# Block-sparse attention and an MLP mixer on one core: zero products in TensorE's gaps up to the first MLP, all transposes on TensorE, block sums by halving, and a new order of all steps

## The chip, the core and the metric

The kernel runs on one core of a Trainium2 chip. A core has five engines that run side by side, each through its own list of instructions in a fixed order: TensorE (PE in the profile; PEld is its weight load), VectorE (DVE), ScalarE (ACT), GpSimd (POOL) and SyncE (SP), which here only issues DMAs. TensorE's clock has two levels, 1.2 and 2.4 GHz; the column "PEclk" is the share of the higher one that was granted. The metric is the device time of one execution in microseconds.

## The reference

Inputs are q, k and v of 4 batches, 8 heads, 768 positions and 64 elements, and four weight matrices. For every head, positions are cut into 12 blocks of 64. A query row attends to its own block and to the three blocks whose mean key has the largest product with the query, as far as they are not in the future.

```python
k_rep = k.reshape(B, H, n_blocks, block, D).mean(axis=3)
gate_scores = np.einsum('bhsd,bhnd->bhsn', q, k_rep)
gate_scores = np.where(causal, gate_scores, -1000000000.0)
top_idx = np.argsort(gate_scores, axis=-1)[..., -top_k:]
...
scores = scale * np.matmul(q, k.transpose(0, 1, 3, 2))
mask = mask & (pos[:, None] >= pos[None, :])
scores = np.where(mask, scores, -1000000000.0)
...
...
xt = x.transpose(0, 2, 1)                      # x: (batch, 768, 512)
h = np.maximum(xt @ w_tok1, 0.0) @ w_tok2      # 768 -> 256 -> 768
u = x + h.transpose(0, 2, 1)
h2 = np.maximum(u @ w_ch1, 0.0) @ w_ch2        # 512 -> 1536 -> 512
return u + h2
```

## The kernel before

The work goes in 16 pairs of heads, four pairs a batch. `pair(p)` records all steps of one pair, `mlp(b)` those of the last two matrix products of a batch, and `block_sums(b, pr)` sums keys over blocks for the four pairs of a batch at once. Nothing runs at that point: each step is an `Op` with a cost on each engine that may do it, the buffers it reads and writes, and a priority `pr`. `Plan.run` then simulates the engines with these costs and lists the steps in the order of their planned starts; that list is what each engine gets, in that order. Priorities come from a pair's due time `T(p)` (7.0 us a pair in the first batch, 13.5 behind) less an offset for each kind of step.

A pair goes as follows. q, k and v are loaded (`q32`, `k32`, `v32`, three buffers each) on SP's queue; in the first batch k, and in all batches q, in pieces of four and two row groups for each head. q is transposed on TensorE in fp32 (line 390, recorded at 479), copied out of PSUM to `QT`, and cast to fp16 by GpSimd into `QA` (line 266 is the helper that writes all such copies). In an early pair (`p < FIRST`, the first four) k goes through TensorE in fp32 too, VectorE reduces the transposed k over each block (line 449) to `ks2`, and the gate is five fp32 products (493). In the other twelve pairs GpSimd casts k to fp16 (463), a DMA transposes it into `KA` (465), VectorE copies one half and the block indicator to their places (468, 470), and the gate uses `block_sums`: one load of the batch's k, four strided reductions on VectorE (398), and a split of the sums and of q into three bf16 parts (`R`, lines 504 and 506), with 15 products (513).

The gate's scores get a bias (518 or 496), the third largest is found (523), and the comparison gives the bias `bn`, which TensorE transposes (537) into extra rows of `QA`; with the indicator in `KA` they make a score of an unselected block very negative. Then for each of the two heads: scores in three groups (559), an exponential on ScalarE (566), a triangular mask on GpSimd (574), the product with V and a column of ones (583), reciprocal and division (586, 590). The two token products follow (601, 615), `u` is their sum with x (618), and u is transposed, by TensorE (631) in the first batch and the last pair and by DMA (622) in the other eleven. `mlp(b)` multiplies u's transpose by `wc1` (651) in 96 products of 384 columns, takes the positive part, and multiplies by `wc2` (669) in 72 products of 512 columns; VectorE adds u (672) and SP stores.

Four PSUM banks, the ring `Rr` (pm in the trace), serve all products but the scores (sc). GpSimd's queue also issues the loads of the weights, from 6 us of the planned time on.

## Time and profile before

| | us |
|---|---|
| median of 3 runs | 313.56 (313.03 to 314.58) |
| profiled execution | 313.72 |
| its span, first to last instruction | 312.0 |
| TensorE busy | 263.2 |
| VectorE busy | 184.1 |
| ScalarE busy | 156.3 |
| GpSimd busy | 108.9 |

TensorE's records overlap: a product's record goes from its start to its modelled end, so a share near 100% says that the engine never ran out of products and not that it worked at its peak. What a product costs in a row of products is the distance of starts. The view of stretches gives busy time of every engine with the number of instructions; the chain of waits gives, piece by piece, what the end hung on; the timeline gives runs of like instructions, and in brackets the idle time before them and what ended it.

### The profile page before, as it was taken

What the parts mean: (1) busy time and instruction counts of PE and PEld (TensorE: products, weight loads), DVE (VectorE), ACT (ScalarE), POOL (GpSimd) and SP (SyncE); (2) the same over time, 40 slices, a digit from 0 to 9 for tenths busy, and PEclk for the clock granted to TensorE, in tenths of its full rate; (3) what the DMA queues carried; (4) which work ended last, traced back from release to release, by engine and by line L of the source; (5) the groups of instructions that cost most, each with busy time, mean ns of one, the idle gap of its engine ahead of it and who ended that gap; (6) DMA issues with size and microseconds to landing.
All of it is one profiled execution on the core that took longest, in us unless ns stands there. A gap on an engine that the chain in (4) does not pass through costs nothing.

```text
span 312.0 us, 6419 instructions
## 1 busy us (share of the span) xinstructions
PE 263.2 (84%) x2437; PEld 175.7 (56%) x2437; DVE 184.1 (59%) x540; ACT 156.3 (50%) x249; POOL 108.9 (35%) x180
## 2 busy tenths in 40 slices
PE   1668987944999887897697999997799999979994
PEld 1537665724575654555554666665575666645551
DVE  6244657497656699788899254579972653320202
ACT  2163756430584548172384537743766477344240
POOL 4325345291174717356442133343652131100000
PEclk9999979685899999999598999999999999999999
DMA  6899999649929999999998152344113121010102
GB/s 121 189 189 189 196 241 216 135 76 156 212 58 186 229 226 202 205 231 227 172 159 175 25 152 56 40 73 106 43 21 56 39 60 28 36 67 0 69 34 101
DMA packets 102071, 38.98 MB, mean 125 GB/s; under 512 B 95012, under 2 KB 98680, under 8 KB 101752
## 3 DMA queue, kind: packets, MB, share of 16 engines
q1 hardware_dynamic: 97840, 34.42, 52.1%
q0 software_dynamic: 3744, 3.93, 8.6%
q8 instruction: 19, 0.31, 0.4%
q10 hardware_dynamic: 456, 0.22, 0.3%
q14 instruction: 12, 0.10, 0.1%
HBM read 31.68 MB, written 6.29 MB: 122 GB/s over the span
## 4 chain that ended last, share of the span: by engine, by line
PE 59%; DVE 29%; ACT 4%; issue 3%; DMA 3%; POOL 1%; SPq 0%; DVEq 0%; ACTq 0%
PE pm L651 13%; PE pm L669 12%; PE sc L559 10%; DVE ksn L398 7%; PE pm L583 4%; PE pm L601 4%; PE sc L669 3%; DVE R L504 3%; PE pm L615 3%; DVE m L523 2%; PE pm L390 2%; PE sc L651 2%; PE pm L493 2%; DVE x L590 2%; ACT E L566 2%
## 5 line engine op out<-in xcount | busy, mean ns | idle before, releaser
L566 ACT ACTIVATE E<-sc 128x1024 f16<-128x1024 f32 (+1 forms) x96 | 84.3, 919 | 31.0 <-PE sc L559 29.7
L574 POOL TENSOR_SCALAR_AFFINE_SELECT E<-E 128x256 f16<-128x256 f16 x96 | 42.5, 446 | 124.4 <-ACT E L566 124.0
L651 PE MATMUL pm<-uT,wc 128*128 128x384 f16 x344 | 66.0, 330 | 3.5 <-DVE u L618 1.1
L669 PE MATMUL pm<-wc,h 128*128 128x512 f16 x240 | 60.9, 379 | 0.8 <-DVE x L590 0.8
L559 PE MATMUL sc<-QA,KA 76*128 76x512 f16 (+7 forms) x256 | 54.3, 335 | 6.2 <-DVE QA L266 4.2
L651 PEld LDWEIGHTS <-wc 128*128 128x128 f16 x384 | 36.3, 99 | 27.9 <-issue 6.3
L658 ACT ACTIVATE h<-pm 128x384 f16<-128x384 f32 x68 | 33.4, 494 | 24.3 <-PE pm L651 24.1
L266 POOL CAST QA<-QT 64x768 f16<-64x768 f32 x32 | 33.3, 1040 | 20.2 <-ACT QT L264 10.3
L559 PEld LDWEIGHTS <-KA 76*128 76x128 f16 (+1 forms) x256 | 25.7, 105 | 25.6 <-issue 8.2
L669 PEld LDWEIGHTS <-h 128*128 128x128 f16 x288 | 26.5, 98 | 24.1 <-issue 1.2
L583 PE MATMUL pm<-VA,E 128*128 128x65 f16 x672 | 29.5, 199 | 5.4 <-POOL E L574 5.2
L583 PEld LDWEIGHTS <-E 128*128 128x128 f16 x672 | 27.5, 102 | 10.8 <-POOL E L574 6.4
L672 DVE TENSOR_TENSOR os<-u,pm 128x512 f32<-128x512 f16 x20 | 13.6, 682 | 17.1 <-PE pm L669 17.1
L618 DVE TENSOR_TENSOR u<-x,pm 128x512 f16<-128x512 f16 (+1 forms) x30 | 15.3, 547 | 12.2 <-PE pm L615 12.1
L398 DVE TENSOR_REDUCE ksn<-kb 96x16 f32<-96x1024 f32 x12 | 22.4, 1893 | 0.0
L264 ACT COPY QA<-pm 12x640 f16<-12x640 f16 x18 | 12.3, 683 | 18.7 <-PE pm L537 16.8
L390 PE MATMUL pm<-id,q 128*128 128x128 f32 x96 | 16.9, 300 | 4.5 <-DMA q<-in_q_dram 3.6
L586 DVE RECIPROCAL rc<-pm 128x6 f32<-128x6 f32 x32 | 6.1, 190 | 24.2 <-PE pm L583 22.6
L605 ACT ACTIVATE h<-pm 128x256 f16<-128x256 f32 x14 | 5.4, 384 | 28.9 <-PE pm L601 28.9
L264 ACT COPY QT<-pm 128x512 f32<-128x512 f32 (+1 forms) x28 | 13.2, 495 | 12.8 <-PE pm L390 11.1
L440 POOL CAST VA<-v 128x768 f16<-128x768 f32 x16 | 14.6, 912 | 13.2 <-DMA v<-in_v_dram 7.5
L601 PE MATMUL pm<-x,w 128*128 128x128 f16 x192 | 15.1, 235 | 4.8 <-DVE x L590 4.8
(70 smaller groups left out, 318.3 us busy)
## 6 DMA issues: line engine op xcount, KB each, us to landing
v<-in_v_dram SPq DMA_DIRECT2D x16, 384.0 KB, 4.0
out_dram<-os SPq DMA_DIRECT2D x24, 256.0 KB, 2.0
k<-in_k_dram SPq DMA_DIRECT2D x24, 192.0 KB, 4.1
kb<-in_k_dram SPq DMA_DIRECT2D x3, 1536.0 KB, 9.1
q<-in_q_dram SPq DMA_DIRECT2D x32, 128.0 KB, 4.7
wc<-in_moe_w_ch_dram POOLq DMA_DIRECT2D x8, 384.0 KB, 6.3
q<-in_q_dram SPq DMA_DIRECT2D x32, 64.0 KB, 3.0
k<-in_k_dram SPq DMA_DIRECT2D x8, 128.0 KB, 3.2
```

Source lines behind the costliest of these rows:

```text
L264: e.copy(out=out, in_=in_)
L266: e.tensor_copy(out=out, in_=in_)
L390: nc.tensor.transpose(out=t[:, 128 * i:128 * i + 128], in_=src.t[:, j0 + i].rearrange("p x d -> p (x d)"), identity=i32)
L398: P.op(dve(1024), lambda i=i: nc.vector.tensor_reduce(out=ksn.t[:, 0, 16 * i:16 * i + 16], in_=kb.t.rearrange("r (t d) -> r d t", d=64)[:, ...
L559: nc.tensor.matmul(out=s.t[:, at:at + 128 * m], lhsT=KA.t[0:K, x, 128 * kk:128 * kk + 128], rhs=QA.t[0:K, x, 128 * q0:128 * (q0 + m)], sta ...
L566: nc.scalar.activation(out=E.t[:, 1024 * g_:1024 * g_ + WIDTH[g_]], in_=s.t[:, 0:WIDTH[g_]], func=AF.Exp, scale=scale)
L574: nc.gpsimd.affine_select(out=o, in_=o, pattern=[[0, 2], [1, 128]], compare_op=ALU.is_ge, fill=0.0, base=0, channel_multiplier=-1)
L583: nc.tensor.matmul(out=t[:, jq, :], lhsT=E.t[:, cc:cc + 128], rhs=VA.t[:, x, kk, :], start=(kk == 0), stop=(kk == jq))
L601: nc.tensor.matmul(out=m1.t[:, 128 * t:128 * t + 128], lhsT=w1[:, j, 128 * t:128 * t + 128], rhs=xp.t[:, j, :], start=(j == 0), stop=(j == ...
L651: nc.tensor.matmul(out=m.t[:, 0:HS], lhsT=wc1[:, c, 128 * f:128 * f + 128], rhs=uT.t[:, c, HS * i:HS * i + HS], start=(c == 0), stop=(c == ...
L658: nc.scalar.activation(out=h2.t[:, f, :], in_=m.t[:, 0:HS], func=AF.Relu)
L669: nc.tensor.matmul(out=m.t, lhsT=h2.t[:, f, 128 * jj:128 * jj + 128], rhs=wc2[:, f, :], start=(f == 0), stop=(f == NFC - 1))
```

## The change

- **Order.** The table `L` replaces the offsets of all priorities, the due times go from 7.0 and 13.5 to 6.85 and 13.33, and the planner's costs change: a factor of 1.05 on three engines, 1.15 on DMA, eight DMA lanes, other costs for single steps.
- **Zero products.** `fill` looks at each planned gap of TensorE before the first MLP product, and puts products of a zero tile with itself there (line 730), into columns of a PSUM bank that nothing reads. There are 107, 47 of them ahead of all else.
- **Early pairs.** The first eight pairs are early instead of four; `block_sums` runs for two batches instead of three.
- **Transposes.** In late pairs k is cast as before, but transposed by TensorE in fp16 (477) and copied from PSUM into both halves of `KA`. u is always transposed by TensorE (650). No DMA transposes are left. `QA` and `KA` are laid out anew, with the extra rows behind the 64 elements for both heads.
- **Loads.** k, q and v come in whole heads (445, 450). The first pair's q is issued on ScalarE's queue. The weights' loads (379) depend on the first pair's `QT`; `wc1` comes in four loads of 128 rows, all of which the first MLP product needs.
- **Block sums.** The sum over a block's 64 rows is made by halving: six adds of 2,048 down to 64 elements (414). The planner may give those of 512 and more to GpSimd.
- **Constants.** The indicator is built on GpSimd and copied by VectorE instead of loaded.

```diff
-    FIRST = PPB
+    FIRST = EARLYP                                   # 8
...
-    EARLY, PACE = 7.0, 13.5
+EARLY, PACE = 6.85, 13.33
...
-        for i in range(4):
-            P.op(dve(1024), lambda i=i: nc.vector.tensor_reduce(
-                out=ksn.t[:, 0, 16 * i:16 * i + 16],
-                in_=kb.t.rearrange("r (t d) -> r d t", d=64)[:, 16 * i:16 * i + 16, :], axis=AX.X, op=ALU.add),
-                rd=[(kb, 0)], wr=[(ksn, i)], pr=pr - 6)
+        n = 2048
+        while n >= 64:
+            c = {"DVE": (n * 1.1 + 75, n * 1.1 + 160)}
+            if n >= 512:
+                c["POOL"] = (n * 1.6 + 75, n * 1.6 + 160)
+            P.op(c, lambda e, n=n: ENG[e].tensor_tensor(out=kb.t[:, 0:n] if n > 64 else ksn.t[:, 0, :], in0=kb.t[:, 0:n], in1=kb.t[:, n:2 * n], op=ALU.add),
+                 rd=[(kb, 0)], wr=[(kb, 0)] if n > 64 else [(ksn, 0)], pr=pr - L["ks"])
+            n //= 2
...
+        for t, src, e, lead in ((k32, ks_, "SP", "kd"), (q32, qs, "ACT" if p == 0 else "SP", "qd")):
+            for x in range(2):
+                P.op({e: (500.0, 1600.0, 768 * 17.6 / 16)}, lambda x=x, t=t, src=src, e=e: ENG[e].dma_start(
+                    out=t.t[:, :, x, :], in_=src[x].rearrange("(j p) d -> p j d", p=128)), wr=[(t, x)], pr=t0 - L[lead] - (99.0 if p == 0 else 0.0))
...
-            P.op({"SP": (700.0, 2200.0, 1500.0)}, lambda: nc.sync.dma_start_transpose(
-                out=KA.t[:, 1, :].rearrange("c (j p) -> c j p", p=128), in_=k16.t.rearrange("p j c -> p (j c)")),
...
+            def ktr(t=t):
+                for j in range(NJ):
+                    nc.tensor.transpose(out=t.t.bitcast(F16)[:, 128 * j:128 * j + 128], in_=k16.t[:, j, :], identity=id16)
+            P.op(pe(*[128] * NJ), ktr, rd=[(k16, 0)], wr=[(t, 0)], pr=t0 - L["kt"])
+            for x in range(2):
+                def kev(e, t=t, x=x):
+                    copy(ENG[e], KA.t[0:64, x, :], t.t.bitcast(F16)[64 * x:64 * x + 64, 0:S])
...
+        if p == 0:
+            weights((QT, 0))
...
-        if p not in UPE:
-            P.op({"SP": (700.0, 2200.0, 1500.0)}, lambda: nc.sync.dma_start_transpose(
...
-    order = P.run(on_slot_end)
+    def fill(o, a, b):
+        if any(x.cls for x in o.bufs):
+            mlp_on.append(1)
+        n = int((b - a) / (54.0 if a > 7000.0 else 104.0) - 1.0)
+        i = min(range(len(pm)), key=lambda i: Rr.avail[i])
+        if mlp_on or n < 2 or Rr.avail[i] > a:
+            return None
+        junk = pm[i][:, 392:512]
...
+                nc.tensor.matmul(out=junk, lhsT=zero, rhs=zero[:, 0:120], start=True, stop=True)
...
+    order = P.run(on_slot_end, fill)
```

TensorE at the start, before; `id_119` is the fp32 identity, `pm` a PSUM bank, the digits after k and q number the buffer, so that k_0 and q_0 belong to the first pair:

```order
L390 MATMUL pm_115<-id_119,k_0_66 128x128 x4
L390 MATMUL pm_116<-id_119,k_0_66 128x128 x2
L390 MATMUL pm_117<-id_119,q_0_63 128x128 x4
L390 MATMUL pm_118<-id_119,q_0_63 128x128 x2
L493 MATMUL pm_115<-ks_0_147,QT_84 128x24 x5
L390 MATMUL pm_116<-id_119,k_1_67 128x128 x4
L390 MATMUL pm_117<-id_119,k_1_67 128x128 x2
L537 LDWEIGHTS bn_153
L537 MATMUL pm_118<-id_120,bn_153 128x128
```

The same engine and place after, with `id_120` the fp32 identity, between the 47 zero products that stand first and the first pair's bias transposes; further zero products stand at the marks:

```order
L730 MATMUL pm_115<-zero 128x120
L399 MATMUL pm_115<-id_120,k_0_66 128x128 x3
L399 MATMUL pm_116<-id_120,k_0_66 128x128 x3
...
L399 MATMUL pm_117<-id_120,q_0_63 128x128 x3
L399 MATMUL pm_118<-id_120,q_0_63 128x128 x3
...
L506 MATMUL pm_115<-ks_0_133,QT_84 128x24 x5
L399 MATMUL pm_117<-id_120,k_1_67 128x128 x3
L399 MATMUL pm_118<-id_120,k_1_67 128x128 x3
...
L399 MATMUL pm_116<-id_120,q_1_64 128x128 x3
L506 MATMUL pm_118<-ks_1_134,QT_85 128x24 x5
L562 MATMUL pm_115<-id_121,bn_135 64x128
```

The second pair's q transposes and its gate have moved ahead of the first pair's bias transposes; before, only its k transposes stood there, and its q behind the first scores.

VectorE where the first block sums stand, before; `ksn` holds the sums of the batch's k in `kb`, `R` the bf16 split of q, `x` the attention's result:

```order
L504 TENSOR_TENSOR R_0_86<-QT_84 128x640
L586 RECIPROCAL rc_170<-pm_117 128x6
L590 TENSOR_TENSOR x_94<-pm_117,rc_170 128x6x64
L506 TENSOR_TENSOR R_0_88<-R_0_86 128x640
L398 TENSOR_REDUCE ksn_160<-kb_74 96x16 x4
L468 COPY KA_79<-KA_79 64x768
L402 COPY ksn_160<-ksn_160 96x64
L470 COPY KA_79<-ind 12x768
L586 RECIPROCAL rc_171<-pm_115 128x6
```

VectorE where its first block sums stand after:

```order
L614 TENSOR_TENSOR x_94<-pm_117,rc_169 128x6x64
L414 TENSOR_TENSOR kb_74<-kb_74 96x1024
L642 TENSOR_TENSOR u_100<-x_94,pm_117 128x384
L642 TENSOR_TENSOR u_100<-x_94,pm_115 128x384
L688 TENSOR_TENSOR os_108<-u_99,pm_116 128x512
L414 TENSOR_TENSOR kb_74<-kb_74 96x256
L288 COPY uT_102<-pm_117 128x384
L414 TENSOR_TENSOR kb_74<-kb_74 96x128
L288 COPY KA_80<-pm_118 64x768
L414 TENSOR_TENSOR ksn_158<-kb_74 96x64
L417 COPY ksn_158<-ksn_158 96x64
```

And GpSimd ahead of and between them, where its two steps of the same sum went:

```order
L598 AFFINE_SELECT E_91<-E_91 128x2x128 x2
L414 TENSOR_TENSOR kb_74<-kb_74 96x2048
L471 CAST k_0_72<-k_2_68 128x768
L451 CAST VA_82<-v_1_70 128x12x64
L414 TENSOR_TENSOR kb_74<-kb_74 96x512
L598 AFFINE_SELECT E_92<-E_92 128x2x128 x3
```

Four reductions in one piece on VectorE, in the second batch, became two adds on GpSimd and four short ones on VectorE with other steps between them, in the third batch; two casts and three masks stand behind the first add on GpSimd.

## Rows read from the trace of the kernel before

**Rows 1.** The page's first part: busy time, share of the span, instructions.
```profile
PE 263.2 (84%) x2437; PEld 175.7 (56%) x2437; DVE 184.1 (59%) x540; ACT 156.3 (50%) x249; POOL 108.9 (35%) x180
```

**Rows 2.** Stretches: length, busy us (instructions) of each engine, granted clock, DMA share, GB/s.
```profile
0.00:33.00 33.00, 20.22 (x118) 15.26 (x119) 14.19 (x57) 12.05 (x17) 12.62 (x30) 1.00 0.94 169
33.00:79.60 46.60, 33.04 (x367) 26.54 (x365) 33.23 (x96) 21.84 (x34) 21.38 (x35) 0.76 0.93 173
79.60:142.00 62.40, 56.92 (x564) 36.96 (x563) 47.30 (x131) 36.47 (x58) 30.60 (x44) 0.99 0.93 194
142.00:169.00 27.00, 19.78 (x199) 13.78 (x197) 23.94 (x69) 14.70 (x26) 12.09 (x17) 0.87 0.95 181
169.00:272.00 103.00, 99.07 (x994) 64.80 (x995) 59.12 (x181) 59.18 (x90) 32.17 (x56) 0.98 0.27 60
272.00:312.00 40.00, 34.17 (x202) 18.35 (x200) 6.37 (x11) 12.10 (x26) 0.00 (x0) 1.00 0.14 53
```

**Rows 3.** Chain of waits: start, length in us, TensorE's pieces of one line.
```profile
39.02 1.12 PE pm L493 x10
86.19 0.87 PE sc L559 x6
87.06 0.67 PE pm L583 x21
87.73 0.65 PE pm L651 x4
89.30 0.66 PE pm L390 x6
92.57 0.67 PE pm L601 x12
95.69 1.94 PE pm L669 x9
```

**Rows 4.** TensorE's timeline at the start: start, length, what [idle before, what ended it].
```profile
5.25 1.51 PE L390 MATMUL pm<-id,k 128*128 128x128 f32 x6 [5.25 <-DMA k<-in_k_dram]
10.38 1.51 PE L390 MATMUL pm<-id,q 128*128 128x128 f32 x6 [3.62 <-DMA q<-in_q_dram]
18.86 1.46 PE L559 MATMUL sc<-QA,KA 128*128 128x512 f16 x4 [1.53 <-DVE QA L266]
```

**Rows 5.** TensorE's timeline: token products of pairs 1, 2, 4, 8, 9, 16; first MLP product.
```profile
33.04 0.84 PE L601 MATMUL pm<-x,w 128*128 128x128 f16 x12
42.81 1.07 PE L601 MATMUL pm<-x,w 128*128 128x128 f16 x12 [0.24 <-DVE x L590]
74.14 1.44 PE L601 MATMUL pm<-x,w 128*128 128x128 f16 x12 [0.81 <-DVE x L590]
79.59 1.49 PE L651 MATMUL pm<-uT,wc 128*128 128x384 f16 x4
142.25 0.83 PE L601 MATMUL pm<-x,w 128*128 128x128 f16 x12
169.14 1.13 PE L601 MATMUL pm<-x,w 128*128 128x128 f16 x12 [2.13 <-DVE x L590]
272.02 0.83 PE L601 MATMUL pm<-x,w 128*128 128x128 f16 x12
```

**Rows 6.** Timelines of VectorE and TensorE at the first block sums.
```profile
65.27 7.21 DVE L398 TENSOR_REDUCE ksn<-kb 96x16 f32<-96x1024 f32 x4
72.90 0.42 PE L403 MATMUL pm<-id,ksn 96*128 96x96 f32 x1 [3.75 <-DVE ksn L402]
```

**Rows 7.** Groups of instructions: out<-in xcount | busy us, mean ns | idle before, releaser.
```profile
L566 ACT ACTIVATE E<-sc 128x1024 f16<-128x1024 f32 (+1 forms) x96 | 84.3, 919 | 31.0 <-PE sc L559 29.7
L398 DVE TENSOR_REDUCE ksn<-kb 96x16 f32<-96x1024 f32 x12 | 22.4, 1893 | 0.0
L504 DVE TENSOR_TENSOR R<-QT 128x640 f32<-128x640 f32 x12 | 13.3, 1106 | 2.0 <-ACT QT L264 1.9
```

**Rows 8.** GpSimd's timeline: two casts of q alone, and two beside R's subtraction.
```profile
38.22 1.70 POOL L266 CAST QA<-QT 64x768 f16<-64x768 f32 x2 [0.58 <-ACT QT L264]
63.13 2.91 POOL L266 CAST QA<-QT 64x768 f16<-64x768 f32 x2 [0.34 <-ACT QT L264]
```

More of the change, by code (lines that the diff above doesn't have):

```diff
@@ L71 @@
     AHEAD = 3000.0
+    LANES = 8
+    SLOW = {"PE": 1.0, "ACT": 1.05, "DVE": 1.05, "POOL": 1.05, "SP": 1.0}
+    DMA = 1.15
     def __init__(self):
@@ L115, in start @@
             t = max(free[e], o.not_before)
+            if e in ("SP", "ACT") and len(o.cost[e]) > 2:
+                t = max(t, lanes[0])
             for d in o.deps:
@@ L145, in run @@
                         t = max(t, dma_free - self.AHEAD)
-                        if any(x[1:] < (o.pr, o.n) and x[0] <= t for x in loads):
+                        if o.pr > -50.0 and any(x[1:] < (o.pr, o.n) and x[0] <= t for x in loads):
                             continue
@@ L163, in run @@
             occ, lat = o.cost[e][:2]
+            occ, lat = occ * self.SLOW[e], lat + occ * (self.SLOW[e] - 1.0)
             o.eng, o.start = e, t
+            if e == "PE" and fill:
+                f = fill(o, free[e], t)
+                if f:
+                    f.n, f.eng, f.start, f.end = -1, e, free[e], t
+                    fillers.append(f)
             free[e] = t + occ
@@ L168, in run @@
                 begin = max(dma_free, t + occ)
-                dma_free = begin + o.cost[e][2]
+                dma_free = begin + o.cost[e][2] * self.DMA
                 o.end = dma_free + lat
+                if e != "POOL":
+                    lanes.pop(0)
+                    lanes.append(o.end)
             for b in o.bufs:
@@ L309 @@
+    zero = sb([128, 128], F16, "zero")
     id32 = sb([128, 128], FP, "id32")
     id16 = sb([128, 128], F16, "id16")
+    ind = sb([NB, S], F16, "ind")
+    warm = sb([128, 1], FP, "warm")
+    cst = sb(list(both.shape), FP, "cst")
+    cstc = nc.inline_tensor(both, name="cstc").ap()
+    gbias, own = cst[:, 0], cst[:, 1]
+    nc.vector.memset(zero, 0.0)
     nc.gpsimd.memset(id32, 0.0)
     nc.gpsimd.affine_select(out=id32, in_=id32, pattern=[[-1, 128]], compare_op=ALU.not_equal, fill=1.0, base=0, channel_multiplier=1)
[L314 to L317 removed]
@@ L354, with weight @@
     W = {}
-    def weight(name, dst, src, cost, pr):
+    HC = DC // 2
+    def weight(name, dst, src, n, each, pr, after):
         b = Buf(None)
         W[name] = (b, 0)
-        P.op(cost, lambda: nc.gpsimd.dma_start(out=dst, in_=src), wr=[(b, 0)], pr=pr, not_before=6000.0)
-    weight("w1", w1, moe_w_tok1.rearrange("(j p) t -> p j t", p=128), swdge(768, 60), 13.0)
-    weight("w2", w2, moe_w_tok2.rearrange("(g p) s -> p g s", p=128), swdge(256, 135), 14.0)
-    HC = DC // 2
-    for i in range(2):
-        for c in range(0, NCC, 2):
-            weight(("wc1", i, c), wc1[:, c:c + 2, HC * i:HC * i + HC],
-                   moe_w_ch1[128 * c:128 * c + 256, HC * i:HC * i + HC].rearrange("(g p) f -> p g f", p=128),
-                   swdge(256, 135), 18.0 + i)
@@ L369, with weights @@
-    for f in range(0, NFC, 3):
-        weight(("wc2", f), wc2[:, f:f + 3, :], moe_w_ch2[128 * f:128 * f + 384, :].rearrange("(g p) c -> p g c", p=128),
-               swdge(384, 98), 25.0 + f / 3)
-    EARLY, PACE = 7.0, 13.5
+        P.op({"POOL": (800.0, 2200.0, n * each / 16.0)}, lambda: nc.gpsimd.dma_start(out=dst, in_=src), rd=[after], wr=[(b, 0)], pr=pr)
+    def weights(after):
+        weight("w1", w1, moe_w_tok1.rearrange("(j p) t -> p j t", p=128), 768, 60, L["w1"], after)
+        weight("w2", w2, moe_w_tok2.rearrange("(g p) s -> p g s", p=128), 256, 135, L["w2"], after)
+        for c in range(NCC):
+            weight(("wc1", c), wc1[:, c, :], moe_w_ch1[128 * c:128 * c + 128, :], 128, 247, L["wc1"] + c, after)
+        for f in range(0, NFC, 3):
+            weight(("wc2", f), wc2[:, f:f + 3, :], moe_w_ch2[128 * f:128 * f + 384, :].rearrange("(g p) c -> p g c", p=128),
+                   384, 98, L["wc2"] + f / 3, after)
@@ L697, in on_slot_end, with zeros @@
             P.quota["mlp"] = 7
-    order = P.run(on_slot_end)
+    mlp_on = []
+    def fill(o, a, b):
[6 more added lines that the diff above has]
+        junk = pm[i][:, 392:512]
+        f = Op()
+        f.cost, f.pr, f.deps = {"PE": (b - a, b - a)}, 0.0, ()
+        def zeros(n=n):
+            for _ in range(n):
+                nc.tensor.matmul(out=junk, lhsT=zero, rhs=zero[:, 0:120], start=True, stop=True)
+        f.fn = zeros
+        return f
+    order = P.run(on_slot_end, fill)
     PLAN.append(P)
```

272 lines of the change are left out of this document (130 added, 142 removed).

## The prediction

> **What bounds the kernel now.** I read the busy shares first, then the stretches, then the chain of waits, then TensorE's and VectorE's timelines. TensorE is busy 84% of the span [rows 1], so the question is what it loses. I price its work at the full clock from runs of back-to-back products in the chain [rows 3]: an MLP product of the first kind 0.65/4 = 0.1625 us, of the second 1.94/9 = 0.216, a head's scores 0.87 x 2,688/2,048 columns = 1.14 (the six products of the row have 2,048 of the head's 2,688), a head's attention-times-V 0.67, a 128-column fp16 product 0.67/12 = 0.056, an fp32 transpose 0.66/6 = 0.11, an fp32 gate 1.12 a pair, and a bf16 gate 0.48 (15 products at 0.67/21). By the program's counts: 384 x 0.1625 + 288 x 0.216 + 32 x 1.14 + 32 x 0.67 + 384 token products, 80 bias and 30 u transposes at 0.056 + 120 x 0.11 + 4 x 1.12 + 12 x 0.48 = 234 us of work in 312 us. So 78 us are lost, and counting the work up to the starts in [rows 5] says where:
> - up to the first MLP product at 79.6: 33.2 of work, 46.4 lost;
> - 79.6 to 142.25: 54.8 of work, 7.9 lost;
> - 142.25 to 169.14: 16.1 of work, 10.8 lost, with VectorE busy 23.9 of 27 [rows 2];
> - 169.14 to 272.02: 96.2 of work, 6.7 lost;
> - to the end: 33.5 of work, 6.5 lost (the last sums, the last store and a gap before the last MLP).
>
> The early loss has three causes. The first scores start at 18.86 because k's transposes run at 5.25 and q's only at 10.38, when q has landed [rows 4]. TensorE is at its lower level: the clock column reads 1.00 up to 33 us, yet six fp32 transposes take 1.51 there against 0.66 later [rows 3, 4], so I go by durations; from 33 to 79.6 the grant is 0.76 [rows 2]. And VectorE sums blocks for 7.2 us from 65.27, for which TensorE waits 3.75 and the pair's token product comes at 74.14 [rows 5, 6].
>
> **TensorE's work after the change.** 24 more fp32 transposes of k cost 2.6, 48 fp16 ones 2.7, 66 more of u 3.7; four gates go from 0.48 to 1.12, 2.6. That makes 245.3. The 107 zero products are 6.0 at the full level, all ahead of the first MLP product. In the new order 49.9 of the total 251.3 stand before that product (five pairs instead of four, and the zeros) and 201.4 behind it. Before, 200.6 stood behind it. So TensorE's work from there on is the same to 1 us, and the time is that product's start plus 201.4 plus what is still lost.
>
> **The start of the first MLP.** q of the first pair is issued on ScalarE's queue beside k on SP's, and the first weight load waits for the first pair. q's transposes move from 10.38 to somewhere between 5.25 + 1.51 and there. But in the new order both transposes and the gate of the second pair stand before the first pair's bias transposes, so TensorE waits for that pair's loads and ScalarE's copies. I take 17.5 for the first scores, between 15.2 (all of the 3.6 us wait for q saved) and 18.9 (nothing). The 47 zeros ahead of the first transposes cost 47 x 0.056 = 2.6 at the full level and 2.3 times that, 6.0, at the lower; starting near 1 us they end at 7 at worst, 1.8 after k was ready, but q and not k ends that wait, so I count 0.
>
> From scores to the first token product it took 14.2 us at the lower level; the one pair that ran at the full level went from 33.04 to 42.81, 9.8 us [rows 5]. I take 9.8: 27.3. Then four pairs. A pair asks TensorE for 6.9 us there (27.4 of work between the first and fifth token products of the new order, zeros included) and ScalarE for 84.3/16 = 5.3 in exponentials alone [rows 7], with copies on top, so 6.9 is a floor; the observed 9.8 is the ceiling. VectorE's block sums are gone here, so I take 8.6, a little nearer to the ceiling, because engines in fixed order wait for each other: 34.4. With a token product and three score products behind it (0.9) the first MLP product starts at 62.6 (55.6 by the floor, 67.4 by the ceiling), 17.0 earlier than before.
>
> **What is still lost behind it.** Block sums cost VectorE 4 x 1.893 = 7.6 us a batch, three times [rows 7]. Now two batches need them, by halving. VectorE's price for a two-input fp32 step is 1,106/640 = 1.73 ns an element [rows 7]; 1,024, 256, 128 and 64 elements cost about 2.6 us, and 512 more (0.9) in one batch. Step 2,048 goes to GpSimd, which has no such row. Its casts of 768 elements, two in 1.70, give 1.1 ns and 2.2 us; VectorE's rate gives 3.5; with the slowing seen when R is subtracted beside two casts, 2.91 against 1.70 [rows 8], 6.1. I take 3.5, the price of the same operation. Masks, casts and hence attention-times-V queue behind it on GpSimd; MLP products that stand between on TensorE cover the 3.5, and without them it is 3.5 a batch, twice.
>
> The Trainium skill's page "GPSIMD Engine Reference" (section "3.1 Elementwise — side-by-side cycle accounting") gives 4,497 ns for a two-input fp32 add of 2,048 elements and keeps such adds on VectorE. That price would add 1.0 us a batch to GpSimd, and 2.0 to the sum if no cover held. No run here shows it yet.
>
> For late pairs, VectorE loses two copies into KA and the R subtractions (1.1 us for the first of two [rows 7]) in the four pairs that are now early; the transposes by DMA go, and their copies out of PSUM (two of 768 for k, two of 384 for u) fall on VectorE and ScalarE, which have room behind 169 (59 of 103 us each [rows 2]) but not before. I keep 4 of the 7.9, 4 of the 10.8 (the batch whose block sums and R steps filled VectorE, with its clock dips) and 2.5 of the 6.7: 10.5, bounds 5 and the old 25.4. The end, 6.5, is unchanged (5.5 to 7).
>
> **Sum.** 62.6 + 201.4 + 10.5 + 6.5 = 281.0 span. The profiled execution took 313.72 for a span of 312.0, 1.7 around it, so 282.7; the median of 313.56 is 0.2 lower, which I leave. A measurement of this kernel tells about 0.5% from no change.
>
> **Rivals.**
> 1. The order holds at its floor: pairs at 6.9 and 5 us lost behind: 55.6 + 201.4 + 5 + 5.5 + 1.7 = 269.2. For it: the clock should be up from the start and the block sums are gone. Against: no interval before came near 6.9. Chance 0.17.
> 2. Losses behind the first MLP stay, since the new PSUM copies take the place of the block sums and GpSimd's adds hold masks: 62.6 + 201.4 + 25.4 + 6.5 + 1.7 = 297.6. For it: VectorE is 76% busy from 79.6 to 142. Chance 0.15.
> 3. The zeros don't do what they say: they stand in gaps that were planned, and the real gaps fall elsewhere, so the clock dips as before. Then the first token product comes at 33.04 - 1.4 = 31.6, four pairs cost (74.14 - 33.04 - 7.2)/3 = 11.3 each, the first MLP starts at 77.7, and the time is 77.7 + 201.4 + 10.5 + 6.5 + 1.7 = 297.8. For it: 60 of the zeros are spread over nine places, 2 to 14 in each. Chance 0.11.
> 4. Slower: TensorE stays at its lower level up to the first MLP. With fp32 and fp16 transposes added there, 49.9 of work at 2.3 times (1.51/0.66) is 115 us, and the time 115 + 201.4 + 10.5 + 6.5 + 1.7 = 335. It decides once the first MLP starts after 93.6. Against: before, MLP-free stretches after 33 us did run at the full level in part. Chance 0.04.
>
> **Chances and range.** My forecast has 0.51; 0.02 is left for no change. Forecast and rivals 1 to 3 are all faster: 0.94. Slower 0.04, same 0.02. The forecast's own range is 275.7 to 291 (floor of the early pace with 10.5 lost behind, its ceiling with 14). For 8 in 10 I cut rival 1 at 269 and take in rivals 2 and 3: 269 to 299.
>
> **What would show it.** Right: six fp32 transposes at about 0.66 within the first 10 us; first scores near 17.5; token products of the first five pairs about 8.6 apart; the first MLP product near 63; no VectorE stretch of 7 us on one line; TensorE gaps behind it summing to about 10. Wrong: a granted clock under 0.9 up to the first MLP, waits for weight loads at that product (its last first-layer part is now issued on GpSimd behind masks of the fifth pair), or masks late behind GpSimd's adds.

## The result and the profile after

The changed kernel took 285.87 us (median of 4 runs, 284.23 to 287.44) where the kernel before took 314.07 in the same rounds (313.03 to 316.44). The ratio is 0.9092, with a 95% interval of 0.9017 to 0.9167: 28.2 us faster. The forecast was 282.7, its range 269 to 299. The profiled execution took 286.3 us, for a span of 284.6. Times are medians over executions; one execution of the last version below (283.55 us) was in a slower state that some executions show, and it is left out.

The page's first part, and the clock's row in its 40 slices, answer to [rows 1]:

```profile
PE 266.0 (93%) x2661; PEld 183.5 (64%) x2661; DVE 177.0 (62%) x542; ACT 163.9 (58%) x264; POOL 112.6 (40%) x182
PEclk9968999999999999997999999999999999999999
```

The stretches, cut at the same events as [rows 2] (first token product, first MLP product, token products of pairs 8, 9 and 16, end); columns as there:

```profile
0.00:33.90 33.90, 28.18 (x269) 24.20 (x270) 24.06 (x87) 17.09 (x28) 16.92 (x37) 0.90 1.12 200
33.90:64.80 30.90, 30.19 (x442) 25.27 (x442) 26.12 (x93) 27.25 (x40) 19.47 (x40) 1.00 1.02 210
64.80:113.70 48.90, 45.67 (x461) 31.32 (x459) 33.33 (x106) 29.78 (x50) 25.45 (x33) 1.00 0.76 147
113.70:134.70 21.00, 16.90 (x166) 10.63 (x164) 15.08 (x34) 8.57 (x12) 10.62 (x11) 0.94 0.58 142
134.70:240.40 105.70, 105.21 (x1107) 71.18 (x1106) 71.16 (x213) 69.12 (x110) 40.11 (x63) 1.00 0.26 66
240.40:284.60 44.20, 39.88 (x228) 20.90 (x227) 7.30 (x12) 12.09 (x26) 0.00 (x0) 1.00 0.15 54
```

TensorE's timeline at the marks themselves, as in [rows 5]: token products of pairs 1, 2 and 5, the first MLP products with their wait for a weight load, token products of pairs 8, 9 and 16:

```profile
33.91 0.83 PE L625 MATMUL pm<-x,w 128*128 128x128 f16 x12
40.59 0.83 PE L625 MATMUL pm<-x,w 128*128 128x128 f16 x12
63.66 0.83 PE L625 MATMUL pm<-x,w 128*128 128x128 f16 x12
64.77 0.65 PE L668 MATMUL pm<-uT,wc 128*128 128x384 f16 x3
67.07 0.34 PE L668 MATMUL pm<-uT,wc 128*128 128x384 f16 x1 [1.65 <-DMA wc<-in_moe_w_ch_dram]
113.66 0.83 PE L625 MATMUL pm<-x,w 128*128 128x128 f16 x12
134.66 1.35 PE L625 MATMUL pm<-x,w 128*128 128x128 f16 x12
240.44 0.83 PE L625 MATMUL sc<-x,w 128*128 128x128 f16 x12 [0.30 <-DVE x L614]
```

With the prediction's prices the work up to these marks gives what TensorE lost in each stretch (length less priced work):

| stretch, by its end | lost before | predicted | lost after |
|---|---|---|---|
| first MLP product | 46.4 | 12.7 | 15.1 |
| token product of pair 8 | 7.9 | 4 | 4.6 |
| token product of pair 9 | 10.8 | 4 | 5.8 |
| token product of pair 16 | 6.7 | 2.5 | 3.2 |
| end | 6.5 | 6.5 | 4.9 |

The first MLP product starts 14.8 us earlier than before (79.59 to 64.77), and the rest is 12.6 shorter (232.4 to 219.8). The work behind that product is the same, 201.4 by price against 200.6, so both halves are losses that went (in all 27.4 of the span).

TensorE's timeline at the start, with the first scores (L583) as its last row here, answers to [rows 4]:

```profile
1.05 4.88 PE L730 MATMUL pm<-zero 128*128 128x120 f16 x47 [1.05 <-DVE zero L339]
6.25 0.84 PE L399 MATMUL pm<-id,k 128*128 128x128 f32 x6 [0.32 <-DMA k<-in_k_dram]
7.04 0.83 PE L399 MATMUL pm<-id,q 128*128 128x128 f32 x6
15.57 1.69 PE L506 MATMUL pm<-ks,QT 128*128 128x24 f32 x10 [2.62 <-DVE ks L467]
17.19 0.74 PE L562 MATMUL pm<-id,bn 128*64 128x128 f16 x5
19.79 1.91 PE L583 MATMUL sc<-QA,KA 76*128 76x512 f16 x6
```

And two stretches of it, as in [rows 2]:

```profile
10.00:15.00 5.00, 2.50 (x26) 2.02 (x25) 3.07 (x16) 2.17 (x5) 2.21 (x4) 1.00 1.32 216
16.25:23.08 6.83, 6.83 (x44) 5.72 (x44) 4.09 (x20) 3.09 (x4) 1.28 (x3) 0.50 1.22 213
```

Six transposes take 0.84 and not 1.51, and q's run at 7.04 and not at 10.38; yet the first scores come at 19.79, later than before's 18.86. Between them stands the second pair's gate, which waits 2.62 for VectorE; the first pair's bias transposes (L562) are behind it in TensorE's list. The wait has a second price: TensorE is busy only half of the 5 us from 10 to 15, and from 16.25 to 23.08 the grant is 0.50, the lower level (1.2 GHz), in spite of the zeros. These six products of the first scores take 1.91, and six of them take 1.04 at 24.34.

One more place, in the stretch that kept the most behind the first MLP product (pair 9's): GpSimd's add of 2,048 elements, VectorE's comparison beside it and at another place, TensorE behind that comparison, and then the other add of 2,048 with a VectorE addition beside it:

```profile
127.10 4.49 POOL L414 TENSOR_TENSOR kb<-kb 96x2048 f32<-96x2048 f32 x1
127.15 4.58 DVE L539 TENSOR_TENSOR ge<-gm,m 128x120 f32<-128x120 f32 x1
113.14 0.27 DVE L539 TENSOR_TENSOR ge<-gm,m 128x120 f32<-128x120 f32 x1
132.18 0.66 PE L562 MATMUL pm<-id,bn 128*64 128x128 f16 x5 [3.99 <-DVE bn L543]
92.11 4.51 POOL L414 TENSOR_TENSOR kb<-kb 96x2048 f32<-96x2048 f32 x1
93.19 0.69 DVE L688 TENSOR_TENSOR os<-u,pm 128x512 f32<-128x512 f16 x1
```

A comparison of 0.27 us, which reads two tiles in SBUF, took 4.58: it started 0.05 behind the add's start and ended 0.14 behind its end, and TensorE waited 3.99 for the bias made from it. Beside the other add VectorE ran four instructions, each with one input in PSUM, and none was longer than elsewhere: the addition above takes 0.69, the mean of its group is 0.68.

### The profile page after: what moved, and what is told of

It reads as the page before. It is cut to its first block, busy times and chain, and to the rows that moved or that the text cites. A ratio compares the mean times of both kernels' runs of the same rounds, so it can differ in the third digit from the quotient of the medians.

```text
span 284.6 us, 6815 instructions
## 1 busy us (share of the span) xinstructions
PE 266.0 (93%) x2661; PEld 183.5 (64%) x2661; DVE 177.0 (62%) x542; ACT 163.9 (58%) x264; POOL 112.6 (40%) x182
## 3 DMA queue, kind: packets, MB, share of 16 engines
q1 hardware_dynamic: 77120, 27.92, 43.6%
## 4 chain that ended last, share of the span: by engine, by line
PE 72%; DVE 10%; DMA 5%; POOL 4%; ACT 4%; issue 2%; SPq 0%; DVEq 0%; ACTq 0%; POOLq 0%
PE pm L668 17%; PE pm L685 16%; PE sc L583 9%; PE pm L607 5%; PE pm L399 4%; DMA wc<-in_moe_w_ch_dram 4%; PE sc L668 3%; PE pm L639 3%; PE sc L685 3%; PE pm L625 2%; DVE ge L539 2%; PE pm L506 2%; POOL kb L414 2%; PE pm L562 2%; ACT E L590 2%
## 5 line engine op out<-in xcount | busy, mean ns | idle before, releaser
L685 PE MATMUL pm<-wc,h 128*128 128x512 f16 x252 | 65.8, 382 | 0.0
L668 PE MATMUL pm<-uT,wc 128*128 128x384 f16 x328 | 61.3, 326 | 1.7 <-DMA wc<-in_moe_w_ch_dram 1.6
L583 PE MATMUL sc<-QA,KA 76*128 76x512 f16 (+3 forms) x256 | 50.7, 310 | 0.9 <-ACT E L590 0.6
L674 ACT ACTIVATE h<-pm 128x384 f16<-128x384 f32 x63 | 30.9, 491 | 27.7 <-PE pm L668 26.7
L288 POOL CAST QA<-QT 64x768 f16<-64x768 f32 x32 | 31.0, 968 | 19.0 <-ACT QT L286 15.1
L583 PEld LDWEIGHTS <-KA 76*128 76x128 f16 x256 | 23.4, 99 | 16.7 <-issue 1.9
L642 DVE TENSOR_TENSOR u<-x,pm 128x384 f16<-128x384 f16 x31 | 15.9, 549 | 10.1 <-PE pm L639 9.8
L614 DVE TENSOR_TENSOR x<-pm,rc 128x384 f16<-128x384 f32 x31 | 17.2, 554 | 0.8
L674 ACT ACTIVATE h<-sc 128x384 f16<-128x384 f32 x14 | 6.5, 489 | 14.3 <-PE sc L668 14.3
L676 DVE TENSOR_SCALAR h<-pm 128x384 f16<-128x384 f32 x19 | 10.4, 553 | 6.9 <-PE pm L668 6.4
L288 DVE COPY QA<-pm 12x640 f16<-12x640 f16 x17 | 8.2, 484 | 9.3 <-ACT QA L286 8.8
L625 PEld LDWEIGHTS <-w 128*128 128x128 f16 x192 | 12.4, 102 | 2.4 <-issue 1.0
```

What stands on the lines that cost most here:

```text
L288: e.tensor_copy(out=out, in_=in_)
L583: nc.tensor.matmul(out=s.t[:, at:at + 128 * m], lhsT=KA.t[:, x, 128 * kk:128 * kk + 128], rhs=QA.t[:, q0:q0 + m, x, :], start=True, stop=True)
L614: P.op(dve(384), lambda a=a, rc=rc, x=x: nc.vector.tensor_tensor(out=xp.t[:, :, 64 * x:64 * x + 64], in0=a.t[:, 0:NJ * 65].rearrange("p (j ...
L625: nc.tensor.matmul(out=m1.t[:, 128 * t:128 * t + 128], lhsT=w1[:, j, 128 * t:128 * t + 128], rhs=xp.t[:, j, :], start=(j == 0), stop=(j == ...
L642: P.op(dve(128 * n), lambda m=m, j0=j0, n=n: nc.vector.tensor_tensor(out=u.t[:, c, j0:j0 + n, :], in0=xp.t[:, j0:j0 + n, :], in1=m.t[:, 0: ...
L668: nc.tensor.matmul(out=m.t[:, 0:HS], lhsT=wc1[:, c, 128 * f:128 * f + 128], rhs=uT.t[:, c, HS * i:HS * i + HS], start=(c == 0), stop=(c == ...
```

## Experiments

Twelve kernels, each timed in the same rounds as the kernel before, whose median was between 313.75 and 314.65 in these.

### Zero products taken out of the changed kernel

```diff
-    order = P.run(on_slot_end, fill)
+    order = P.run(on_slot_end)
```

> The changed kernel without its 107 zero products; every engine's order is otherwise the same. Theory (the zeros keep TensorE's clock up early): the first 33 us run at the lower level as in the kernel before, six fp32 transposes take 1.5 us again instead of 0.84, the first MLP product moves from 64.8 to about 69, and the time is 290 to 292. Rival (the early stretch waits for loads, VectorE and ScalarE, not for TensorE): the clock falls just as low but the first MLP product stays within 1 us and the time within 0.5% of the changed kernel's 285.9.

Measured 285.63 us (285.13 to 287.13), ratio 0.91 (0.9043 to 0.9157). TensorE's timeline at the first transposes, and at the first MLP product:

```profile
6.32 1.51 PE L399 MATMUL pm<-id,k 128*128 128x128 f32 x6 [6.32 <-DMA k<-in_k_dram]
7.62 1.48 PE L399 MATMUL pm<-id,q 128*128 128x128 f32 x6
65.34 0.65 PE L668 MATMUL pm<-uT,wc 128*128 128x384 f16 x3
```

Without zeros the transposes run at the lower level (1.51 against 0.84) and the first recorded grant at the upper level is at 25.6; still the first MLP product comes only 0.6 later, and the end at the same time: the rival's forecast. In this execution the work of the new order brought the upper level without zeros, 2.5 us after the kernel with zeros had come back to it (23.08). A run without zeros further down (adds on VectorE) shows that this does not always come so early.

### Zero products put into the kernel before

```diff
...
-    order = P.run(on_slot_end)
+    mlp_on = []
+
+    def fill(o, a, b):
...
+    order = P.run(on_slot_end, fill)
```

> The kernel before, with zero products alone: the same filling of planned gaps up to the first MLP product, no other edit. Theory (zeros raise the clock): TensorE is at its upper level from about 6 us on instead of 33, the first token product comes 2 to 4 us earlier, and the time is 308 to 311. Rival (early the chain runs through VectorE, loads and GpSimd): the clock rises and the time stays at 313 to 315, or grows by what zeros add where the real gap was shorter than the planned one.

Measured 308.99 us (308.7 to 309.11), ratio 0.9834 (0.9778 to 0.989). Stretches from 33 us to the first MLP product and to 142:

```profile
33.00:74.80 41.80, 36.44 (x585) 32.56 (x584) 33.18 (x96) 20.94 (x33) 21.25 (x35) 1.00 1.12 198
74.80:142.00 67.20, 60.30 (x618) 39.84 (x615) 50.63 (x148) 38.55 (x62) 32.38 (x46) 1.00 0.96 199
```

The planner found room for 375 zeros here, against 107 in the changed kernel. The grant is 1.00 where it was 0.76 [rows 2], and the first MLP product starts at 74.83 instead of 79.59. The start is not held throughout (0.50 from 8.47 to 18.71), and the first token product comes 1 us earlier, not the 2 to 4 expected. So zeros do hold the clock from 18.71 on, and are worth 5 us where TensorE has holes; in the new order they are worth less.

### The halving adds all on VectorE

```diff
...
+            def halve(e, n=n):
+                ENG[e].tensor_tensor(out=kb.t[:, 0:n] if n > 64 else ksn.t[:, 0, :], in0=kb.t[:, 0:n], in1=kb.t[:, n:2 * n], op=ALU.add)
+            P.op(c, halve,
...
+        if o.fn.__name__ == "halve":
+            o.eng = "DVE"
```

> The changed kernel with the three adds of the halving that went to GpSimd issued on VectorE at the same places of the order; nothing else differs. Theory (GpSimd's add of 2,048 elements holds VectorE): in the changed kernel the comparison on VectorE took 4.58 us instead of 0.28, over just the 4.49 us of the add, and TensorE waited 3.99 for it. On VectorE the add costs about 3.6 (1.82 for 1,024), the comparison is back at 0.28, masks no longer queue, and 2 to 4 us go: 282 to 284. Rival (it is VectorE's time either way): the add sits ahead of the same comparison for 3.6 instead of 4.5, and the time stays within 1 us of 285.9.

Measured 281.83 us (281.36 to 284.0), ratio 0.8967 (0.8906 to 0.9029): 4.0 us less than the changed kernel. VectorE's timeline at the first of the two adds of 2,048 and at the comparison (now line 541) near the second:

```profile
92.93 2.28 DVE L415 TENSOR_TENSOR kb<-kb 96x2048 f32<-96x2048 f32 x1
128.55 0.28 DVE L541 TENSOR_TENSOR ge<-gm,m 128x120 f32<-128x120 f32 x1
```

The add takes 2.28 on VectorE where GpSimd took 4.49, the comparison is back at 0.28, and the 3.99 wait is gone. But not all of the 4.0 is the adds'. The two profiled executions differ by 3.3 in span (284.6 against 281.3), and 1.4 of that is there at the first MLP product, ahead of both sums. The start of that stretch, and the product:

```profile
17.41:20.82 3.41, 3.41 (x22) 2.63 (x22) 2.18 (x14) 1.71 (x3) 0.00 (x0) 0.50 1.04 223
63.38 0.49 PE L670 MATMUL pm<-uT,wc 128*128 128x384 f16 x2
```

TensorE's list up to there is the same in five of these kernels. In the two whose grant was 0.50 for 6.83 us (the changed kernel and the strided reductions below) the first MLP product starts at 64.77 and 64.81; in the three with 3.41 us of it (this one, and the two with u by DMA and zeros below) at 63.26 to 63.39. So the 1.4 goes with the clock of the execution and not with the edit, and 1.9 of the profiled 3.3 lies behind the first MLP product, where the edit is.

### Strided reductions instead of halving

```diff
-        n = 2048
-        while n >= 64:
...
+        for i in range(4):
+            P.op({"DVE": (1850.0, 1935.0)}, lambda i=i: nc.vector.tensor_reduce(
...
```

> The changed kernel with the four strided reductions of the kernel before in place of the halving, for the two batches that still need block sums; order listed anew, the same up to the first MLP product. Theory (halving is worth little once the first batch that needs it has MLP products beside it, and GpSimd's add has its own price): VectorE carries 7.6 us a batch, gates of the third and fourth batch come late once or twice, and the time is 284 to 289, near the changed kernel's 285.9. Rival (the strided sums were what held TensorE behind 142 in the kernel before): 5 us a batch more are lost, 291 to 296.

Measured 284.74 us (284.14 to 286.02), ratio 0.9036 (0.8965 to 0.9107). Halving as the change has it gives nothing against the old reductions (285.87). On VectorE alone it gives 2.9 by the medians (281.83 against 284.74), but the profiled executions differ by 1.7 in span, of which 1.4 is ahead of the first MLP product (64.81 against 63.38) with the clock as above. What the halving itself gives is therefore not shown; behind that product it is 0.3.

### The first pair's bias ahead of the second pair's gate

```diff
-                    rd=[(t, 0)], wr=[(ksa, i)], pr=t0 - L["kr"])
+                    rd=[(t, 0)] + ([(fixed, "first")] if p == 1 else []), wr=[(ksa, i)], pr=t0 - L["kr"])
...
-            P.op(pe(*[128] * 5), btr, rd=[(bn, 0), (bn, 1)], wr=[(bt, 0)], pr=t0 - L["b"])
+            P.op(pe(*[128] * 5), btr, rd=[(bn, 0), (bn, 1)], wr=[(bt, 0)] + ([(fixed, "first")] if p == 0 else []), pr=t0 - L["b"])
```

> The changed kernel, where the planner must place the first pair's bias transposes before the second pair's block reductions on VectorE, and so before its gate. Theory (the 3.3 us saved on loading q were lost to the order): first scores near 15 instead of 19.8, and the time 281 to 283. Rival (the start is not what the first MLP waits for: its last weights land at 67.1 whatever the pairs do, with DMA busy throughout): first scores near 15, the first MLP product still at 65 to 67, the time within 1 us of 285.9.

Measured 285.3 us (284.17 to 287.51), ratio 0.909 (0.9023 to 0.9157). TensorE's timeline has the first scores and the first MLP product at

```profile
16.22 1.03 PE L583 MATMUL sc<-QA,KA 76*128 76x512 f16 x6
65.91 0.86 PE L668 MATMUL pm<-uT,wc 128*128 128x384 f16 x4
```

The scores start 3.6 earlier, the MLP 1.1 later, as the rival had it. Without the 2.62 wait the grant stays at 1.00 from the first record (5.96) past the first MLP product. But the planner listed the order anew: 54.1 us of priced work stand ahead of the first MLP product instead of 49.9, with 151 zeros for 107 (2.5 of the 4.2), and in the changed kernel TensorE is already busy 43.6 of the 45 us from 20 on. So the run shows that an earlier start alone does not bring the MLP forward; it does not test the order of these steps by itself.

### Four early pairs in the changed kernel, and eight in the kernel before

```diff
-EARLYP = 8
+EARLYP = 4
```

> The changed kernel with four early pairs instead of eight, so that block sums run for three batches again; the planner lists the order anew, zeros included. Theory (the eight early pairs remove the first block sums and R splits ahead of the first MLP): VectorE and GpSimd carry one more halving there (4.5 for GpSimd's add, about 6 for the rest) and eight more R subtractions, the first MLP product comes at 70 or later, and the time is 292 to 297. Rival (TensorE is what counts, and it has about 4 us less of fp32 work): 282 to 287.

Measured 300.93 us (300.18 to 302.64), ratio 0.955 (0.9483 to 0.9617): 15 us more than the changed kernel, above both expectations, and still 13.7 less than the kernel before. Timelines of GpSimd, VectorE and TensorE in front of the first token product:

```profile
36.20 4.52 POOL L414 TENSOR_TENSOR kb<-kb 96x2048 f32<-96x2048 f32 x1
40.75 3.58 DVE L414 TENSOR_TENSOR kb<-kb 96x1024 f32<-96x1024 f32 x4 [2.79 <-POOL kb L414]
42.88 0.27 PE L607 MATMUL pm<-VA,E 128*128 128x65 f16 x3 [0.80 <-POOL E L598]
46.57 1.09 PE L625 MATMUL pm<-x,w 128*128 128x128 f16 x12
```

The sums of the second batch are back ahead of the MLP: VectorE waits 2.79 for GpSimd's add and works 3.58 more on the sums, masks queue behind the add, the first token product comes at 46.57 and the first MLP product at 76.15 instead of 64.77. The planner put 245 zeros here instead of 107, 7.7 us more by price; whether they cost anything in these gaps is not shown. Then I set the same constant alone in the kernel before:

```diff
-    FIRST = PPB
+    FIRST = 8
```

> The kernel before with its one constant for early pairs at eight instead of four: two batches of block sums, no other edit, its own table of priorities, its own DMA transposes and its own costs. Theory: in the changed kernel four early pairs more were worth 15 us (300.93 against 285.87), because the block sums of 7.2 us on VectorE and the bf16 splits leave the part before the first MLP; that hangs on the pairs and not on the new table, so the kernel before should gain most of it too: 298 to 304, with the first MLP product at 66 to 72 instead of 79.6. Rival: the early pairs pay only with priorities that were listed anew for them; the old offsets and due times leave TensorE waiting elsewhere, and fp32 transposes and gates of pairs 4 to 7 are added work (2.6 and 2.6 us): 309 to 316.

Measured 316.03 us (314.85 to 317.41, 10 runs), ratio 1.0058 (1.0031 to 1.0085): slower, if by little. One stretch of this kernel, a VectorE reduction in it, and TensorE's longest wait:

```profile
142.00:169.00 27.00, 20.40 (x205) 14.32 (x203) 22.66 (x94) 15.34 (x22) 9.05 (x16) 0.65 0.36 83
144.14 1.85 DVE L398 TENSOR_REDUCE ksn<-kb 96x16 f32<-96x1024 f32 x1
141.52 0.22 PE L513 MATMUL pm<-ksp,QT 128*128 128x72 bf16 x1 [5.85 <-DVE os L672]
```

The first MLP product comes 2.6 earlier (77.03 against 79.59). But by 135 us all MLP products of the first batch are used up (96 of the first kind, 72 of the second), and none runs before 183; the split of one batch's sums, reductions of the next, R steps and gates then go through VectorE with no MLP product beside them, TensorE waits 5.85 in one piece, and the grant falls to 0.65. My theory for this run failed: the eight early pairs pay only together with the rest of the change. They are worth 15 us there and cost 1.7 in the kernel before, so they have no price of their own.

### u transposed by DMA in eleven pairs, as before

```diff
-        t = Buf(Rr)
+        if 4 <= p < NP - 1:
+            P.op({"SP": (700.0, 2200.0, 1500.0)}, lambda: nc.sync.dma_start_transpose(
+                out=uT.t[:, c, :].rearrange("c (j p) -> c j p", p=128), in_=u.t[:, c].rearrange("p j d -> p (j d)")),
+                rd=[(u, (c, 0)), (u, (c, 1))], wr=[(uT, (c, 0)), (uT, (c, 1))], pr=t2 + 0.4)
+        else:
+            t = Buf(Rr)
...
```

> The changed kernel with u transposed by DMA again in the eleven pairs where the kernel before did so; order listed anew. Theory (behind the first MLP product the time is TensorE's work plus a loss that stays): 66 transposes of 0.056 go, 3.7 us, with the 22 copies out of PSUM, and the time is 281 to 284. Rival (the transposes wait on SP behind loads that wait for buffers, as the 37 us of SP's waits for u show in the kernel before): MLP products come late and the time is 286 to 292.

Measured 278.78 us (278.35 to 279.22), ratio 0.884 (0.8785 to 0.8895): 7.1 less than the changed kernel, more than the 3.7 of work that leaves TensorE and better than both expectations. One stretch, from the first MLP product to pair 9's token product, of this kernel:

```profile
63.30:128.40 65.10, 62.44 (x605) 41.75 (x603) 43.20 (x133) 38.60 (x62) 31.45 (x42) 0.97 0.95 182
```

It is 65.1 long against 69.9 in the changed kernel (the third and fourth stretches above), with DMA 0.95 busy instead of 0.71. Part of this is the planner's: with other transposes it put the second add of 2,048 on VectorE, so the 3.99 wait is gone here too. It put the add of 1,024 behind it on GpSimd instead, and the same comparison met that one:

```profile
139.06 2.34 POOL L414 TENSOR_TENSOR kb<-kb 96x1024 f32<-96x1024 f32 x1
140.19 1.70 DVE L539 TENSOR_TENSOR ge<-gm,m 128x120 f32<-128x120 f32 x1
```

It started 1.13 into the add and took 1.70: the hold a second time, in another kernel, at another size.

### Both of the edits that gained

```diff
-        t = Buf(Rr)
+        if 4 <= p < NP - 1:
...
+        if o.fn.__name__ == "halve":
+            o.eng = "DVE"
```

> The changed kernel with both edits that gained alone: u of the eleven pairs 4 to 14 transposed by DMA (alone 278.78) and the halving adds of 512 and 2,048 named to VectorE (alone 281.83), against 285.87. Theory: the two remove different losses, TensorE work and copies out of PSUM on the one side and GpSimd's 4.49 us adds that hold VectorE and the masks on the other; the adds' 4.0 come off again: 274 to 276. Rival: both give TensorE the same slack, as no zeros, adds and bias order together gave less than the adds alone, so that the second edit adds little: 277 to 279. If the time is above 279.5 the adds on VectorE stand in the way of something that the DMA transposes make early.

Measured 277.58 us (276.62 to 278.45), ratio 0.8833 (0.8804 to 0.8862), the fastest version of this study. VectorE's timeline at the two adds of 2,048:

```profile
91.48 2.28 DVE L415 TENSOR_TENSOR kb<-kb 96x2048 f32<-96x2048 f32 x1
137.02 2.28 DVE L415 TENSOR_TENSOR kb<-kb 96x2048 f32<-96x2048 f32 x1
```

The second edit adds 1.2 and not 4.0, as the rival had it: of the 7.1 above, some 3 was not the transposes', but this same wait and the clock at the start (1.5 at the first MLP product). The DMA transposes alone are then worth 281.83 - 277.58 = 4.2, about the 3.7 of work. These two versions have the same clock at the start and the same first MLP product (63.38 and 63.39), so this difference is the cleanest here.

### Three edits at once, and zeros taken from the better versions

No zeros, adds on VectorE and the bias order together:

```diff
...
+                    rd=[(t, 0)] + ([(fixed, "first")] if p == 1 else []), wr=[(ksa, i)], pr=t0 - L["kr"])
...
+    order = P.run(on_slot_end)
...
+            o.eng = "DVE"
```

> The changed kernel with three edits: no zero products, GpSimd's adds of the halving on VectorE, and the first pair's bias transposes ahead of the second pair's gate. Theory (the zeros cost where the gaps have become short, and with the bias first the 3 us saved at the start were given back to 44 more zeros and two us of other work moved ahead): 278 to 281. Rival (the edits overlap, and the loads set the start of the first MLP): 281 to 283, as with the adds alone.

Measured 284.64 us (283.76 to 285.48), ratio 0.9025 (0.8965 to 0.9086). That is 2.8 above the adds alone and fits neither expectation. Two more runs were to say which edit costs: the adds on VectorE without zeros,

```diff
-    order = P.run(on_slot_end, fill)
+    order = P.run(on_slot_end)
...
+            o.eng = "DVE"
```

> The changed kernel with the halving adds of 512 and 2,048 named to VectorE and without the zero products; the first pair's bias stays where it is. No zeros, adds and bias order together gave 284.64 (283.76 to 285.48), 2.8 more than the adds alone (281.83), and either the missing zeros or the bias order must have cost it. Theory: the bias order did, since the zeros were worth nothing in the changed kernel (285.63 without, 285.87 with): 281 to 282.5. Rival: the zeros are worth 2 to 3 us once the wait behind GpSimd's add no longer stands at the end of their gain: 283.5 to 285, with the first MLP product 1 to 3 us later than the 63.38 of the adds alone.

Measured 283.32 us (282.27 to 285.03), ratio 0.9034 (0.8985 to 0.9084). TensorE's timeline of the profiled execution (285.03 us) at the fourth pair's k transposes, and at the first MLP product:

```profile
29.30 1.49 PE L399 MATMUL pm<-id,k 128*128 128x128 f32 x6
68.12 0.65 PE L670 MATMUL pm<-uT,wc 128*128 128x384 f16 x3
```

The list up to this product is that of the first run without zeros, but here the first recorded grant at the upper level is at 33.8 and not at 25.6, six transposes still take 1.49 at 29.30, and the first MLP product comes 4.7 later than with zeros (63.38). The end comes only 2.0 later (283.3 against 281.3 of span): a microsecond lost ahead of the first MLP product is not a whole one at the end. Then the fastest version without zeros:

```diff
...
+        if 4 <= p < NP - 1:
...
-    order = P.run(on_slot_end, fill)
+    order = P.run(on_slot_end)
...
+            o.eng = "DVE"
```

> The kernel with u of pairs 4 to 14 transposed by DMA and all halving adds on VectorE (277.58, 276.62 to 278.45) without the zero products. Theory: the same as with them, 277 to 278.3, with the upper clock level some us later at the start and the first MLP product within 1 us of the one with zeros (63.4). Rival: the zeros buy 2 to 5 us here as they did in the kernel before (5 us): 279.5 to 282.5.

Measured 278.83 us (277.41 to 279.24, 4 runs), ratio 0.8871 (0.8822 to 0.892). Removing the zeros thus cost -0.2, 1.5 and 1.3 us in three versions, and the runs with and without them overlap each time: once the order is new the zeros are worth between 0 and 2 us, not 5, and the traces above differ in when the clock rose without them. The 2.8 divides into 1.5 for the zeros and 1.3 for the bias order, each inside the scatter of its runs; which of them is real stays open.

## Why the prediction was right, and where its steps were not

**The sum.** It gave a span of 281.0 against 284.6: 2.2 too little up to the first MLP product (62.6 against 64.77), 1.4 too little behind it (17.0 lost against 18.4). The frame held: the same work behind the first MLP product, so that its start and the losses make the time. The two are not independent, though: in the run above that started its MLP 4.7 later, the rest was 2.7 shorter.

**Two terms of the start were wrong, against each other.**
- The first scores were put at 17.5 and came at 19.79, outside the bounds 15.2 to 18.9. Counting q's load as the only thing that changed, I bounded it by "nothing gained", although the text itself said that the second pair's gate now stands ahead; its 2.62 wait, and the lower clock level behind it, were not priced.
- From there to the first token product I took 9.8 us, the distance of two token products of before. It took 14.1. The order has 11.2 us of priced work between those two points in the changed kernel (transposes, gates and scores of later pairs that were moved ahead), so 9.8 was below the work alone, before any wait and before the lower level that TensorE kept until 23.08. The term that failed is this one: I used a pace as a latency. The token product came at 33.91 and not at 27.3, as late as before.
- The four pairs behind it took 29.8 (33.91 to 63.66), 7.4 each, against 8.6 predicted and a floor of 6.9. The work moved ahead in the step before is missing here, and TensorE is busy 30.19 of 30.9. The two errors, 6.6 too early and 4.6 too slow, cancelled all but 2, so that 62.6 came out close says nothing for either step.

**Two readings of rows.** "2.3 times" for the lower level divides the length of a run of six transposes (1.51) by the distance of starts of such a run at the upper level (0.66). Like with like it is 1.51 against 0.84, 1.8 times, so that the sign "about 0.66" came true as 0.84, and rival 4's 115 us should have been about 90. And 1.73 ns an element came from the mean of twelve subtractions that took 0.81 to 1.48 us; the shortest has 1.26.

**The first weight loads** were named among what would show the forecast wrong. TensorE did stand idle for 1.65 before the fourth MLP product. Where the MLP started 1.1 later, with the bias first, four products ran in a row with no such wait.

**Losses behind.** The four stretches behind the first MLP product came out within 1.8 of what was kept for them. The largest error, pair 9's stretch (5.8 against 4), has the 3.99 wait behind GpSimd's add in it. I priced the add at 3.5 by VectorE's row; it took 4.49 and 4.51, within the bounds 2.2 to 6.1. I let MLP products cover it: that held for the first add and failed for the second. I named masks and casts as what queues behind it, and missed VectorE: the comparison with two inputs that started beside it was held for its whole length. The figure of the Trainium skill's page "GPSIMD Engine Reference" (section "3.1 Elementwise — side-by-side cycle accounting"), 4,497 ns, agrees with the trace, and so does its advice to keep such adds on VectorE: they took 2.28 there, and the time fell by 4.0, of which about 2 is theirs by the traces. The hold is told in the Trainium skill's page "SBUF — State Buffer" (section "SBUF: two separate sides"): a VectorE instruction with two SBUF inputs and a GpSimd instruction that reads SBUF share a port pair that one holds for its whole instruction. The 4.58 beside 4.49 agrees, and so do the 1.70 beside the add of 1,024 and the four instructions with an input in PSUM, which kept their lengths beside the first add.

**The rivals.** Rival 1, the floor (269.2), missed by a first MLP product 9.2 later than its 55.6 and by 7.9 more lost behind; the pace itself came within 0.5 of it. Rival 2 was right that GpSimd's adds would hold something, and wrong in size: the old 25.4 fell to 13.6 without the end. Rival 3 argued that the zeros would not hold the clock. They raise it at the start (six transposes take 0.84 with them and 1.51 without), and it did fall once, behind the gate's wait; but the rival's price of 15 us was wrong in another way: without any zeros the first MLP product came at 65.34 and 68.12, not 77.7. The grant dips of before came from TensorE's holes, since filling them with zeros alone took the grant from 0.76 to 1.00, and the new order closes most of them with work. Rival 4 did not occur.

**u on TensorE.** I priced it at 3.7 and it cost 4.2 (277.58 against 281.83 on the same footing). That price was right, and is the part of the change that was a loss; the DMA transposes had no cost that these runs show.

**What the gain is.** The early pairs are worth 15 us on top of the rest of the change (300.93 against 285.87) and cost 1.7 without it (316.03). The rest of the change without them is worth 13.7 (300.93 against 314.65 in the same rounds). Within that rest, the zeros add 0 to 2, the adds on GpSimd cost 2 to 4, and u on TensorE costs 4. The new priorities and costs, the loads in whole heads and on ScalarE's queue, k's transposes on TensorE and the constants were not tested apart, so which of them carries the 13.7 is open.

## What to carry to other kernels

Price the start of a pipeline by the work that the new order lists between two marks, not by the distance of marks further on; a pace is no latency. Filling a clock's holes with empty products paid where holes were left (5 us before), and was worth 0 to 2 us once real work filled them, so it is best tried last. Before a difference of a few microseconds is put down to an edit, compare the two traces at a mark that the edit cannot reach: here 1.4 us of several differences stood there already. When a step is given to GpSimd to relieve VectorE, look at which VectorE instructions run beside it: here a comparison of two inputs of 120 elements waited as long as an add of 2,048.

## What was not expected of the hardware

- An add of 2,048 fp32 elements on GpSimd held a VectorE comparison of 0.27 us for 4.58, and an add of 1,024 held it for 1.70; VectorE instructions with an input in PSUM ran beside the other add of 2,048 at their usual lengths.
- With the same list of TensorE's products, the grant at the start was 0.50 for 6.83 us in two traces and for 3.41 in three, and without zeros the upper level was first recorded at 25.6 in one and at 33.8 in another; the first MLP product moved with it, by 1.4 and by 2.8 us.
- VectorE adds 2,048 elements in 2.28 us, 1.11 ns an element, less than the 1.73 that [rows 7] gave for a subtraction of two fp32 inputs (640 elements in a mean of 1.106); the estimate of the halving from that row was over half too high.
- The clock's column reads 1.00 up to its first record also in the kernel without zeros (25.6 us there), while six fp32 transposes take 1.51 against 0.84 with zeros; durations of a known row tell the level where the column does not.
